# Landmark attention beside a feed-forward stream: two attention products on smaller array tiles, one conversion on more partitions, and a reordered slot table

## The chip, the cores and the metric

The kernel runs on one core of a Trainium2 chip. The metric is the device time of one execution in microseconds (us); the time before is the median of three runs. Times of instructions come from one profiled execution.

## The reference, cut to what matters

Three blocks follow one another on 8 batches of 576 positions and 512 features: attention through 32 landmarks per head (8 heads of 64), a feed-forward block with a low-rank mix over positions, and a second block with a Fourier mix.

```python
q_lm, k_lm = means of q and k over 18 positions each       # 32 landmarks
A  = softmax(q @ k_lm.T);  Bm = softmax(q_lm @ k_lm.T);  C = softmax(q_lm @ k.T)
Z  = Bm.T / (norm1(Bm) * norminf(Bm) + 1e-6)
for _ in range(6): Z = 2 * Z - Z @ Bm @ Z                  # Newton
x  = A @ Z @ C @ v                                         # attention
u  = x + (x.transpose @ U @ V).transpose                   # U: 576x32, V: 32x576
y  = u + relu(u @ w_ch1) @ w_ch2                           # 512 -> 2048 -> 512
# then the Fourier block, ending in another 512 -> 2048 -> 512
```

U, V and the weights arrive as 64-bit floats and are converted on the chip.

## The kernel before, in words

Each of the two 512-2048-512 products is done in two passes, with half of the hidden units each. A pass streams nine chunks of 512 positions (`Mlp.stream`). A chunk has 16 steps: in steps 0 to 7 `up` computes one block of hidden units (12 matmuls of 128x512, lines 241 to 243), steps 8 to 15 are halves of the four down blocks (12 matmuls each, lines 285 to 287). The numbers are split into a high and a low part, which makes three matmuls of one product.

The attention of the eight batches is interleaved with pass 0, and a few small steps of it stand after the matmuls of each step of the stream. `Batch.steps` gives each of them a slot number; `Slots` hangs them onto the steps, and within a slot they are issued in the order of the table. Every engine and the DMA queue on SyncE run their instructions in the order written (`manual_schedule`). Batch b starts 12 steps before chunk b-1, so slot r of it falls on step (r + 4) mod 16 of a chunk. Batch 0 and the first 12 slots of batch 1 lie in a prologue ahead of the first chunk, in which `filler` matmuls (line 962) stand in each slot.

The attention works on pairs of heads: k and q lie as head features on partitions 0 to 63 and 64 to 127. `scores(g)` (slots 6 and 8) multiplies landmark queries with all keys, two heads per half g, into two PSUM banks "c" of 288 columns; the maximum is taken on VectorE and the exponential on ScalarE. `newton` (slots 14 to 19) is one step of the iteration on eight 32x32 blocks. `query_t` and `query_tail` (slots 16, 17) transpose the softmax of the queries into the tile `at`. `heads` and `rank` (slots 20, 21) build the tile `W`. `mix(i)` (slots 22 to 25) is W times `at` for 128 output features: before, the contraction has 128 rows, of which 64 belong to two heads, 32 to the low-rank part (V lies there in `at`, and U'A times W in `W`), and 32 are zeros. Its two banks "n" are copied by ScalarE into a tile `u1T`, stored by a DMA of ScalarE, and split into high and low parts for the stream (`hand_head`).

The weights of pass 0 are converted one after the other by `convert`: five VectorE operations on 128x512 (lines 96, 97, 100, 103, 106), two on ScalarE, two on GpSimd. U and V go first through `from_f64` (lines 61 to 72). The generator `convs` chains them: two of its pieces per slot in the prologue from slot 4 on, four per step in chunk 0. The feed-forward needs weight i at step i.

Of the kernel before, what the change touches and what calls it, by code (L numbers as in the profile page):

```python
# [22 lines left out]
LM, W = 32, 18  # L23
# [16 lines left out]
def body(ctx: ExitStack, tc: tile.TileContext, qT, kT, vn, mU, mV, w11, w12, w21, w22,  # L40
# [273 lines left out]
    staged = [[dram.tile([P, 2, 512], F32, name=f"d{p}_{i}") for i in range(2 * HM)] for p in range(4)]  # L314
    BANKS = {"c": 2, "b": 1, "n": 2}

    def attention_constants(cp, t):
# [12 lines left out]
        nc.gpsimd.memset(t["at"][0:32, 1:4:2, :], 0.0)  # L330

    def attention_setup(t, pool, cvp):
        uraw = cvp.tile([P, 1024], U32, name="wraw", bufs=2)[:, 0:10 * R].bitcast(U64).rearrange(
            "p (t r) -> p t r", r=R)
        nc.sync.dma_start(uraw[:, 0:4, :], mU[0:512].rearrange("(t p) r -> p t r", p=P))
        for e in range(2):
            nc.sync.dma_start(uraw[64 * e:64 * e + 64, 4, :], mU[512:576])
        yield 1
        yield from from_f64(cvp, t["U"].rearrange("p t r -> p (t r)"), uraw.rearrange("p t r -> p (t r)"), 5 * R)
        vst = pool.tile([P, S], F32, name="u1T", bufs=2)[0:R]  # L340
        for n in range(3):
            c = slice(n * S // 3, (n + 1) * S // 3)
            vraw = cvp.tile([P, 1024], U32, name="wraw", bufs=2)[0:R, 0:2 * S // 3].bitcast(U64)
            nc.sync.dma_start(vraw, mV[:, c])
            yield 1
            yield from from_f64(cvp, vst[:, c], vraw, S // 3, R)
        for e in range(2):
            for g in range(2):
                nc.scalar.copy(t["at"][64 - 32 * e:96 - 32 * e, 2 * g + e, :], vst)
            yield 1  # L350

    class Batch:
# [100 lines left out]

        def scores(self, g):

            qb = self.t["qb"]
            E = self.E[g] = self.pool.tile([P, S], F32, name="E", bufs=2)
            m, s, x = self.stat(2), self.stat(2), self.stat(1)
            if g == 0:
                self.rC = self.stat(2)  # L460
            pss = []
            for n in range(2):
                ps = self.bank("c")
                for e in range(2):
                    nc.tensor.matmul(ps[self.EJ[e], 0:HS], qb[:, 2 * g + e, :],  # L465
                                     self.k[:, 2 * g + e, n * HS:(n + 1) * HS], start=True, stop=True)
                pss.append(ps)
            for n in range(2):
                nc.vector.tensor_reduce(m[:, n:n + 1], pss[n][:, 0:HS], axis=AX.X, op=ALU.max)
            nc.vector.tensor_scalar(x, m[:, 0:1], m[:, 1:2], -self.scC, op0=ALU.max, op1=ALU.mult)  # L470
            for n in range(2):
                nc.scalar.activation(E[:, n * HS:(n + 1) * HS], pss[n][:, 0:HS], AF.Exp, bias=x, scale=self.scC,
                                     accum_out=s[:, n:n + 1])
            r = self.rC[:, g:g + 1]
            nc.vector.tensor_scalar(r, s[:, 0:1], s[:, 1:2], 1e-9, op0=ALU.add, op1=ALU.add)
            nc.vector.reciprocal(r, r)

# [74 lines left out]
        def query_t(self, g):  # L552
            at = self.t["at"]
            ps = self.bank("c")
            for i in range(4):
                nc.tensor.transpose(ps[:, i * P:(i + 1) * P], self.A[:, 512 * g + i * P:512 * g + (i + 1) * P], ident_sb)
            nc.scalar.copy(at[0:64, 2 * g, 0:512], ps[0:64])
            nc.scalar.copy(at[64:P, 2 * g + 1, 0:512], ps[64:P])

        def query_tail(self):  # L560
            at = self.t["at"]
            ps = self.bank("b")
            for g in range(2):
                nc.tensor.transpose(ps[0:64, g * P:(g + 1) * P], self.A[:, 1024 + 64 * g:1088 + 64 * g], ident_sb)
            v = ps[0:64, 0:2 * P].rearrange("p (g c) -> p g c", g=2)
            nc.scalar.copy(at[0:64, 0:4:2, 512:S], v[:, :, 0:64])
            nc.scalar.copy(at[64:P, 1:4:2, 512:S], v[:, :, 64:P])

# [34 lines left out]
        def heads(self):  # L603
# [7 lines left out]
            v = ps[:, 0:P].rearrange("p (g c) -> p g c", g=2)  # L611
            for h in range(4):
                sl, e, c = slice(32 * h, 32 * h + 32), h // 2, slice(64 * (h % 2), 64 * (h % 2) + 64)
                if e:
                    nc.vector.tensor_copy(W_[sl, e:4:2, c], v[sl])
                else:
                    nc.scalar.copy(W_[sl, e:4:2, c], v[sl])

        def rank(self):
# [3 lines left out]
            for g in range(2):  # L623
                for e in range(2):
                    sl, o = self.EJ[e], slice(64 - 32 * e, 96 - 32 * e)
                    nc.tensor.matmul(ps[o, P * g:P * g + P], self.au[sl, g, :], W_[sl, 2 * g + e, :], start=True,
                                     stop=True)
            v = ps[:, 0:2 * P].rearrange("p (g c) -> p g c", g=2)
            nc.scalar.copy(W_[64:96, 0:4:2, :], v[64:96])
            nc.vector.tensor_copy(W_[32:64, 1:4:2, :], v[32:64])  # L630

        def mix(self, i):
            W_, at, u = self.t["W"], self.t["at"], u1[self.b]
            if self.b == 0:
                self.mlp.hand_tail(0, i)
            u1T = self.pool.tile([P, S], F32, name="u1T", bufs=2)
            pss = []
            for n in range(2):
                ps = self.bank("n")
                nc.tensor.matmul(ps[:, 0:HS], W_[:, i, :], at[:, i, n * HS:(n + 1) * HS], start=True, stop=True)  # L640
                pss.append(ps)
            nc.scalar.copy(u1T[:, 0:HS], pss[0][:, 0:HS])
            nc.scalar.copy(u1T[:, HS:S], pss[1][:, 0:HS])
            nc.scalar.dma_start(u[rows(i), :], u1T)
            self.mlp.hand_head(self.b, i, u1T)

        def steps(self, after):
# [15 lines left out]
            yield from ((22 + i, lambda i=i: self.mix(i)) for i in range(4))  # L663
            if after:
# [248 lines left out]
    with pool("mm") as mp, pool("pm", space=PSUM) as pm:  # L913
# [34 lines left out]
        with pool("aa") as ap_, pool("ac") as ac, pool("cv0") as cv0, pool("pt", space=PSUM) as psb:  # L948
# [139 lines left out]
```

## Time and profile before

| quantity | us |
|---|---|
| median of three runs (1944.62 to 1950.64) | 1946.72 |
| profiled execution | 1947.52 |
| its span, first to last instruction | 1945.7 |
| TensorE busy in the span | 1888.9 (97%) |
| VectorE busy | 932.1 (48%) |
| ScalarE busy | 554.7 (29%) |
| GpSimd busy | 372.0 (19%) |

The 1.8 us by which the profiled time exceeds its span lie around the first and the last instruction. Busy times overlap, and a matmul in the pipeline counts as busy until its modelled end. A matmul on 4-byte floats that aren't split shows as two rows of the trace: `mix(i)`, two matmuls in the program, is four rows.

### The profile page before, as it was taken

The numbers are of one execution on the slowest core, as the hardware profiler recorded it, in microseconds if no ns is written. First come the engines' busy times: TensorE is split into PE (matmuls) and PEld (weight loads), VectorE is DVE, ScalarE is ACT, GpSimd is POOL, SyncE is SP. The second block draws the span as 40 slices with busy tenths as digits, with TensorE's granted clock in tenths as the row PEclk, the third lists the DMA queues.
The fourth block names the chain that finished last, engine by engine and source line by source line (L and its number), as shares of the span: only waits on it lengthen the run. The fifth ranks groups of instructions, "written<-read, shape, count | busy, mean of one in ns | idle before, by whom it ended". The sixth has DMA issues, their size and how long they took to land.

```text
span 1945.7 us, 29294 instructions
## 1 busy us (share of the span) xinstructions
PE 1888.9 (97%) x11840; PEld 1531.0 (79%) x11840; DVE 932.1 (48%) x1636; ACT 554.7 (29%) x1173; POOL 372.0 (19%) x357
## 2 busy tenths in 40 slices
PE   6879999999999999999999999999999999999998
PEld 5656777777788887887888888888888888888887
DVE  6885566556432334556474364554522133333333
ACT  3433333333331222333233243433322211111110
POOL 2450122112111122123232132312211000010000
PEclk9999999999999999999999999999999999999999
DMA  6424435444346533444352852442422743223332
GB/s 242 142 74 152 153 114 172 158 149 139 102 133 210 179 114 128 143 147 165 128 163 85 301 173 79 136 157 85 146 92 97 233 134 110 93 92 98 98 98 76
DMA packets 150232, 267.14 MB, mean 137 GB/s; under 512 B 23536, under 2 KB 81744, under 8 KB 150096
## 3 DMA queue, kind: packets, MB, share of 16 engines
q1 hardware_dynamic: 145488, 255.82, 39.6%
q10 hardware_dynamic: 4608, 9.44, 1.3%
q8 instruction: 93, 1.52, 0.3%
q14 instruction: 43, 0.35, 0.1%
HBM read 171.62 MB, written 93.59 MB: 136 GB/s over the span
## 4 chain that ended last, share of the span: by engine, by line
PE 86%; DVE 7%; ACT 2%; DMA 2%; issue 1%; SPq 0%; ACTq 0%; POOL 0%; DVEq 0%
PE ps L285 13%; PE ps L287 13%; PE ps L286 13%; PE ps L241 12%; PE ps L243 12%; PE ps L242 12%; PE ps_n L640 1%; DMA U<-x 1%; PE ps_f L76 1%; PE ps_f L77 1%; PE ps_f L78 1%; DVE g L246 1%; PE ps_c L465 1%; PE ps L962 1%; DVE cva L106 1%
## 5 line engine op out<-in xcount | busy, mean ns | idle before, releaser
L285 PE MATMUL ps<-g,w 128*128 128x512 f32 x1152 | 461.7, 401 | 0.0
L241 PE MATMUL ps<-x,w 128*128 128x512 f32 x1152 | 459.4, 399 | 0.0
L287 PE MATMUL ps<-g,w 128*128 128x512 f32 x1152 | 451.1, 392 | 1.2 <-DVE g L246 1.2
L286 PE MATMUL ps<-g,w 128*128 128x512 f32 x1152 | 450.5, 391 | 0.0
L243 PE MATMUL ps<-x,w 128*128 128x512 f32 x1152 | 449.8, 390 | 0.0
L242 PE MATMUL ps<-x,w 128*128 128x512 f32 x1152 | 449.6, 390 | 0.0
L246 DVE SCALAR_TENSOR_TENSOR g<-ps,g 128x512 fp32r<-128x512 f32 x288 | 198.5, 690 | 476.2 <-ACT g L245 475.7
L245 ACT ACTIVATE g<-ps 128x512 fp32r<-128x512 f32 x288 | 171.8, 597 | 716.4 <-PE ps L243 716.0
L285 PEld LDWEIGHTS ps<-g,w 128*128 128x128 f32 x1152 | 217.1, 188 | 51.3 <-issue 5.9
L287 PEld LDWEIGHTS ps<-g,w 128*128 128x128 f32 x1152 | 217.2, 189 | 48.8 <-DVE g L246 2.1
L241 PEld LDWEIGHTS ps<-x,w 128*128 128x128 f32 x1152 | 216.5, 188 | 49.0 <-issue 0.3
L243 PEld LDWEIGHTS ps<-x,w 128*128 128x128 f32 x1152 | 216.5, 188 | 46.5
L286 PEld LDWEIGHTS ps<-g,w 128*128 128x128 f32 x1152 | 217.4, 189 | 43.5
L242 PEld LDWEIGHTS ps<-x,w 128*128 128x128 f32 x1152 | 216.8, 188 | 42.6
L294 DVE TENSOR_TENSOR xf<-ps,xf 128x512 f32<-128x512 f32 x108 | 74.5, 690 | 241.9 <-PE ps L287 210.1
L52 POOL TENSOR_TENSOR x<-xf,x 128x512 fp32r<-128x512 f32 (+7 forms) x70 | 85.5, 1228 | 529.0 <-ACT x L51 493.8
L104 POOL TENSOR_TENSOR cvp<-cvp,cva 128x512 f32<-128x512 f32 x64 | 85.8, 1341 | 401.7 <-DVE cvp L103 401.5
L52 POOL TENSOR_TENSOR stg<-cva,stg 128x512 fp32r<-128x512 f32 x48 | 68.3, 1424 | 98.6 <-ACT stg L51 98.0
L51 ACT CAST x<-xf 128x512 fp32r<-128x512 f32 (+7 forms) x140 | 75.1, 575 | 0.4
L101 ACT ACTIVATE wraw<-wraw 128x512 f32<-128x512 f32 x56 | 38.0, 678 | 97.8 <-DVE cva L97 97.8
L106 DVE SCALAR_TENSOR_TENSOR cva<-wraw,cvp 128x512 f32<-128x512 f32 x56 | 51.0, 911 | 29.6 <-POOL cvp L104 29.6
L52 DVE TENSOR_TENSOR x<-xf,x 128x512 fp32r<-128x512 f32 (+7 forms) x70 | 50.1, 715 | 29.9 <-ACT x L51 26.9
(278 smaller groups left out, 1745.8 us busy)
## 6 DMA issues: line engine op xcount, KB each, us to landing
wraw<-w SPq DMA_DIRECT2D x56, 512.0 KB
d<-stg SPq DMA_DIRECT2D x48, 512.0 KB
w<-d SPq DMA_DIRECT2D x48, 512.0 KB
y<-xf SPq DMA_DIRECT2D x72, 256.0 KB
xf<-y SPq DMA_DIRECT2D x72, 256.0 KB
u<-u1T ACTq DMA_DIRECT2D x32, 288.0 KB
U<-x SPq DMA_DIRECT2D x8, 1152.0 KB
u<-U SPq DMA_DIRECT2D x8, 1152.0 KB
```

The costliest lines, as they stand in the source:

```text
L51: nc.scalar.copy(hi, src)
L52: (eng or nc.vector).tensor_tensor(lo, src, f32(hi), op=ALU.subtract)
L104: nc.gpsimd.tensor_tensor(pf, pf, af, op=ALU.add)
L241: nc.tensor.matmul(ps, wh, xh, start=k == 0, stop=False)
L242: nc.tensor.matmul(ps, wl, xh, start=False, stop=False)
L243: nc.tensor.matmul(ps, wh, xl, start=False, stop=k == 3)
L245: nc.scalar.activation(g[:, 0, :], ps, AF.Relu)
L246: nc.vector.scalar_tensor_tensor(out=g[:, 1, :], in0=ps, scalar=0.0, in1=f32(g[:, 0, :]), op0=ALU.max, op1=ALU.subtract)
L285: nc.tensor.matmul(ps, wh, gh, start=k == 0, stop=False)
L286: nc.tensor.matmul(ps, wl, gh, start=False, stop=False)
L287: nc.tensor.matmul(ps, wh, gl, start=False, stop=k == HM - 1)
L294: nc.vector.tensor_tensor(res[d], ps, res[d], op=ALU.add)
```

## The change

`mix` becomes `mix(g, n)`: the zero rows go, each head pair gets a contraction of 64 rows (32 attention rows and 32 low-rank rows), and four matmuls of 64x64 by 288 columns write two banks. `scores` becomes one step (slot 6) for both halves, with contraction over one head's 64 features, 32 landmarks and 512 columns, on eight tiles of 64x32; the last 64 columns of all eight heads go to bank "b" as 128x32 tiles. `at` and `W` get a new layout, so `query_t` and `query_tail` copy in quarters of 32 partitions, and `rank` runs on 32x32 tiles. V is converted in one go on 96 partitions and put into `at` by twelve DMAs in slot 14. Newton's steps are first in their slots.

```diff
-        t["W"] = cp.tile([P, 4, P], F32, name="W")
-        nc.gpsimd.memset(t["W"], 0.0)
-        nc.gpsimd.memset(t["at"][96:P, 0:4:2, :], 0.0)
-        nc.gpsimd.memset(t["at"][0:32, 1:4:2, :], 0.0)
+        t["W"] = cp.tile([P, 4, 64], F32, name="W")
...
-        for n in range(3):
-            vraw = cvp.tile([P, 1024], U32, name="wraw", bufs=2)[0:R, 0:2 * S // 3].bitcast(U64)
-            nc.sync.dma_start(vraw, mV[:, c])
-            yield 1
-            yield from from_f64(cvp, vst[:, c], vraw, S // 3, R)
-        for e in range(2):
-            for g in range(2):
-                nc.scalar.copy(t["at"][64 - 32 * e:96 - 32 * e, 2 * g + e, :], vst)
-            yield 1
+        for n in range(3):
+            nc.sync.dma_start(vraw[R * n:R * n + R], mV[:, n * S // 3:(n + 1) * S // 3])
+        yield 1
+        yield from from_f64(cvp, t["vst"], vraw, S // 3, 3 * R)
+    def place_v(t):
+        for n in range(3):
+            src = t["vst"][R * n:R * n + R].unsqueeze(1).to_broadcast([R, 2, S // 3])
+            for h in range(4):
+                nc.sync.dma_start(t["at"][32 * h:32 * h + 32, 1 - h % 2:4:2, n * S // 3:(n + 1) * S // 3], src)
...
+            pss, tl = [self.bank("c") for _ in range(2)], self.bank("b")
+            for g in range(2):
+                for h, sl in enumerate(self.QUARTERS):
+                    r, c = self.EJ[h % 2 ^ g], slice(32 * (h % 2), 32 * (h % 2) + 32)
+                    nc.tensor.matmul(pss[g][sl], qb[r, 2 * g + h // 2, c], self.k[r, 2 * g + h // 2, 0:512], ...)
+            for g in range(2):
+                for h, sl in enumerate(self.QUARTERS):
+                    nc.tensor.matmul(tl[sl, 64 * g:64 * g + 64], qb[:, 2 * g + h // 2, c],
+                                     self.k[:, 2 * g + h // 2, 512:S], ...)
...
-            nc.scalar.copy(at[0:64, 2 * g, 0:512], ps[0:64])
-            nc.scalar.copy(at[64:P, 2 * g + 1, 0:512], ps[64:P])
+            for h, sl in enumerate(self.QUARTERS):
+                nc.scalar.copy(at[sl, 2 * g + h % 2, 0:512], ps[sl])
...
-        def mix(self, i):
-                nc.tensor.matmul(ps[:, 0:HS], W_[:, i, :], at[:, i, n * HS:(n + 1) * HS], start=True, stop=True)
+        def mix(self, g, n):
+            if n == 0:
+                self.u1T = [self.pool.tile([P, S], F32, name="u1T", bufs=UB) for _ in range(2)]
+            pss = [self.bank("n") for _ in range(2)]
+            for c, cl in enumerate(self.EJ):
+                for r, sl in enumerate(self.EJ):
+                    nc.tensor.matmul(pss[r][cl, 0:HS], W_[sl, 2 * g + c, :], at[sl, 2 * g + c, q], ...)
+            for r in range(2):
+                nc.scalar.copy(self.u1T[r][:, q], pss[r][:, 0:HS])
+            if n == 1:
+                for r in range(2):
+                    nc.scalar.dma_start(u[rows(i), :], self.u1T[r])
+                    self.mlp.hand_head(self.b, i, self.u1T[r])
...
-            yield from ((6, lambda: self.scores(0)), (8, lambda: self.scores(1)), (10, lambda: self.scores_t(0)),
+            yield from ((14 + i, lambda i=i: self.newton(i)) for i in range(6))
+            yield from ((6, self.scores), (10, lambda: self.scores_t(0)),
...
-            yield from ((14 + i, lambda i=i: self.newton(i)) for i in range(6))
...
+            slots.add(FIRST, [(14, lambda: place_v(t))])
```

Here `EJ` are the two halves of the partitions and `QUARTERS` the four quarters; UB is 3, so `u1T` has three buffers in place of two.

The program's order shows three places. The first is TensorE in the prologue, from batch 1's `scores` and batch 0's `heads` on (L962 are the fillers). Before:

```order
L609 MATMUL ps_n<-ry,Bf 32x64 x8
L465 MATMUL ps_c<-k__364,qb 64x288 x4
L962 MATMUL ps<-ident_sb 128x128 x6
L626 MATMUL ps_n<-W,au 32x128 x4
L962 MATMUL ps<-ident_sb 128x128 x6
L640 MATMUL ps_n<-at,W 128x288 x2
L431 MATMUL ps_b<-dg,bones_sb 128x128
L465 MATMUL ps_c<-k__364,qb 64x288 x4
```

The same place now:

```order
L617 MATMUL ps_n<-ry,Bf 32x64 x8
L463 MATMUL ps_c<-k__390,qb 32x512 x8
L468 MATMUL ps_b<-k__390,qb 32x64 x8
L971 MATMUL ps<-ident_sb 128x128 x6
L628 MATMUL ps_n<-W,au 32x64 x8
L971 MATMUL ps<-ident_sb 128x128 x6
L644 MATMUL ps_n<-at,W 64x288 x4
L430 MATMUL ps_b<-dg,bones_sb 128x128
```

The second `scores` (L465) is gone from the step of `norms` (L431, now L430), the first has become L463 and L468, and `mix` has four matmuls instead of two.

The second place is VectorE in the prologue after `residue` (L450, now L449; lines 61 to 72 are U and V, 96 to 106 the weights, 507 and 536 belong to `values` and `query`). Before:

```order
L450 SCALAR_TENSOR_TENSOR ry<-ps_b,st,istack_sb 128x32 x2
L61 TENSOR_SCALAR cva<-wraw 32x192
L62 SCALAR_TENSOR_TENSOR cva<-wraw,cva 32x192
L65 TENSOR_SCALAR cvp<-cva 32x192
L68 SCALAR_TENSOR_TENSOR cvp<-wraw,cvp 32x192
L72 SCALAR_TENSOR_TENSOR u1T<-wraw,cvp 32x192
L61 TENSOR_SCALAR cva<-wraw 32x192
L62 SCALAR_TENSOR_TENSOR cva<-wraw,cva 32x192
L507 TENSOR_TENSOR st<-st 128x2
```

Now:

```order
L72 SCALAR_TENSOR_TENSOR u1T<-wraw,cvp 96x192
L449 SCALAR_TENSOR_TENSOR ry<-ps_b,st,istack_sb 128x32 x2
L96 TENSOR_SCALAR cva<-g 128x512
L97 SCALAR_TENSOR_TENSOR cva<-g,cva 128x512
L100 TENSOR_SCALAR cvp<-cva 128x512
L103 SCALAR_TENSOR_TENSOR cvp<-g,cvp 128x512
L96 TENSOR_SCALAR cva<-g 128x512
L97 SCALAR_TENSOR_TENSOR cva<-g,cva 128x512
L106 SCALAR_TENSOR_TENSOR cva<-g,cvp 128x512
L100 TENSOR_SCALAR cvp<-cva 128x512
L103 SCALAR_TENSOR_TENSOR cvp<-g,cvp 128x512
L543 TENSOR_REDUCE sm<-ps_c 128x16
```

V is finished here, and the weights follow at once; before, they began six slots further on. Five weights were finished (L106) ahead of the first hidden block (L246), now eight.

The third place is VectorE at the end of the conversions in chunk 0. Before, the last of the 16 (L106 without a further L96) stands in step 10, between two down blocks (L294):

```order
L294 TENSOR_TENSOR xf<-ps,xf 128x512
L630 COPY W<-ps_n 32x2x128
L52 TENSOR_TENSOR x<-xf,x 128x64
L408 TENSOR_REDUCE st<-ps_b 128x2
...
L469 TENSOR_REDUCE st<-ps_c 128x1 x2
L470 TENSOR_SCALAR st<-st 128x1
L475 TENSOR_SCALAR st<-st 128x1
L476 RECIPROCAL st<-st 128x1
L106 SCALAR_TENSOR_TENSOR cva<-wraw,cvp 128x512
L294 TENSOR_TENSOR xf<-ps,xf 128x512
```

Now it stands behind the last hidden block (L246), which ends step 7:

```order
L246 SCALAR_TENSOR_TENSOR g<-ps,g 128x512
L608 TENSOR_TENSOR ry<-ps_n,ry 128x2x64
L383 TENSOR_REDUCE ls<-q__1343 128x64
L106 SCALAR_TENSOR_TENSOR cva<-wraw,cvp 128x512
L619 COPY W<-ps_n 128x256
L52 TENSOR_TENSOR x<-xf,x 128x64
L294 TENSOR_TENSOR xf<-ps,xf 128x512
```

Steps 8 to 15 of chunk 0 hold no conversion any more.

## Rows read from the trace of the kernel before

**Rows 1.** The profile's first part: span, and busy time of TensorE

```profile
span 1945.7 us, 29294 instructions
PE 1888.9 (97%) x11840; PEld 1531.0 (79%) x11840; DVE 932.1 (48%) x1636; ACT 554.7 (29%) x1173; POOL 372.0 (19%) x357
```

**Rows 2.** Busy time by stretch (stretch, length, PE, PEld, DVE, ACT, POOL, clock, DMA)

```profile
20.00:30.00 10.00, 10.00 (x221) 9.26 (x221) 4.45 (x18) 3.16 (x9) 0.58 (x1) 1.00 0.38 131
79.00:123.00 44.00, 34.58 (x494) 26.07 (x492) 36.98 (x67) 16.82 (x36) 20.49 (x18) 0.96 0.41 134
123.00:169.00 46.00, 38.12 (x202) 26.92 (x199) 29.09 (x64) 16.25 (x43) 14.77 (x16) 0.89 0.30 104
169.00:234.00 65.00, 64.98 (x689) 49.29 (x688) 36.35 (x82) 23.08 (x61) 10.68 (x16) 1.00 0.42 133
```

**Rows 3.** Waits of TensorE, first 160 us (total, times, longest)

```profile
PE ps_n L595 <- DVE ry L600: 10.4, 6, 3.1
PE ps_n L640 <- ACT u1T L642: 3.8, 2, 2.6
```

**Rows 4.** Groups of VectorE instructions from 79 to 151 us (busy, mean ns)

```profile
L106 DVE SCALAR_TENSOR_TENSOR cva<-wraw,cvp 128x512 f32<-128x512 f32 x8 | 5.6, 705 | 0.0
L97 DVE SCALAR_TENSOR_TENSOR cva<-wraw,cva 128x512 uint32<-128x512 uint32 x8 | 5.5, 693 | 0.3
L103 DVE SCALAR_TENSOR_TENSOR cvp<-wraw,cvp 128x512 f32<-128x512 uint32 x8 | 5.5, 692 | 0.3
L100 DVE TENSOR_SCALAR cvp<-cva 128x512 uint32<-128x512 uint32 x11 | 4.6, 419 | 0.0
```

**Rows 5.** VectorE in order of time: two operations on V, the last conversion

```profile
16.69 0.23 DVE L61 TENSOR_SCALAR cva<-wraw 32x192 uint32<-32x192 uint32 x1
16.96 0.35 DVE L62 SCALAR_TENSOR_TENSOR cva<-wraw,cva 32x192 uint32<-32x192 uint32 x1
...
149.96 0.67 DVE L106 SCALAR_TENSOR_TENSOR cva<-wraw,cvp 128x512 f32<-128x512 f32 x1
```

**Rows 6.** TensorE in order of time around a `mix` alone (start, length)

```profile
346.48 0.39 PE L287 MATMUL ps<-g,w 128*128 128x512 f32 x1
346.71 1.13 PE L640 MATMUL ps_n<-at,W 128*128 128x288 f32 x4
...
347.91 0.39 PE L286 MATMUL ps<-g,w 128*128 128x512 f32 x1
```

**Rows 7.** The same view around `mix` and `scores` in one step

```profile
341.45 0.39 PE L287 MATMUL ps<-g,w 128*128 128x512 f32 x1
341.67 1.13 PE L640 MATMUL ps_n<-at,W 128*128 128x288 f32 x4
342.74 1.19 PE L465 MATMUL ps_c<-k__3322,qb 128*64 128x288 f32 x8
...
344.19 0.40 PE L286 MATMUL ps<-g,w 128*128 128x512 f32 x1
```

**Rows 8.** The same view: 32x32 tiles, `newton` alone and a product of `residue`

```profile
311.52 0.39 PE L243 MATMUL ps<-x,w 128*128 128x512 f32 x1
311.84 0.53 PE L595 MATMUL ps_n<-ry 32*32 32x96 f32 x16
...
312.64 0.39 PE L242 MATMUL ps<-x,w 128*128 128x512 f32 x1
...
356.76 0.33 PE L447 MATMUL ps_b<-BT 32*32 32x32 f32 x16
```

**Rows 9.** The same view: `rank` on two 64x32 tiles, then `kernel`

```profile
337.99 0.63 PE L626 MATMUL ps_n<-W,au 64*32 64x128 f32 x8
338.54 0.33 PE L402 MATMUL ps_b<-kb,qb 128*32 128x32 f32 x16
```

**Rows 10.** ScalarE copies into `at` and one exponential of `scores`

```profile
L557 ACT COPY at<-ps_c x16: 563/566/577, 43.4 to 521.7; 64x512 f32<-64x512 f32 x16
...
345.58 0.50 ACT L472 ACTIVATE E<-ps_c,st 128x288 f32<-128x288 f32 x1 [1.54 <-DVE st L470]
```

More of the change, by code (lines that the diff above doesn't have):

```diff
@@ L315, in body @@
     BANKS = {"c": 2, "b": 1, "n": 2}
+    UB = 3
     def attention_constants(cp, t):
@@ L452, in residue, with scores @@
                                                op1=ALU.add)
-        def scores(self, g):
+        def scores(self):
             qb = self.t["qb"]
[L457 to L476, printed above, removed]
@@ new lines, in scores @@
+            for g in range(2):
+                for h, sl in enumerate(self.QUARTERS):
+                    c = slice(32 * (h % 2), 32 * (h % 2) + 32)
+                    nc.tensor.matmul(tl[sl, 64 * g:64 * g + 64], qb[:, 2 * g + h // 2, c],
+                                     self.k[:, 2 * g + h // 2, 512:S], start=True, stop=True, skip_group_check=True)
+            for g in range(2):
+                nc.vector.tensor_reduce(m[:, 0, g:g + 1], pss[g], axis=AX.X, op=ALU.max)
+            nc.vector.tensor_reduce(m[:, 1, :], tl[:, 0:P].rearrange("p (g c) -> p g c", g=2), axis=AX.X, op=ALU.max)
@@ new lines, in scores @@
+            nc.vector.tensor_tensor(x, m[:, 0, :], m[:, 1, :], op=ALU.max)
+            nc.vector.tensor_scalar_mul(x, x, -self.scC)
+            for g in range(2):
+                E = self.E[g] = self.pool.tile([P, S], F32, name="E", bufs=2)
+                nc.scalar.activation(E[:, 0:512], pss[g], AF.Exp, bias=x[:, g:g + 1], scale=self.scC,
+                                     accum_out=sm[:, 0, g:g + 1])
+                nc.scalar.activation(E[:, 512:S], tl[:, 64 * g:64 * g + 64], AF.Exp, bias=x[:, g:g + 1],
+                                     scale=self.scC, accum_out=sm[:, 1, g:g + 1])
@@ L478, in scores_t @@
+            nc.vector.tensor_tensor(self.rC, sm[:, 0, :], sm[:, 1, :], op=ALU.add)
+            nc.vector.tensor_scalar_add(self.rC, self.rC, 1e-9)
+            nc.vector.reciprocal(self.rC, self.rC)
         def scores_t(self, g):
@@ L563, in query_tail @@
             for g in range(2):
[L564 to L567, printed above, removed]
+                for e, sl in enumerate(self.EJ):
+                    nc.tensor.matmul(ps[sl, 64 * g:64 * g + 64], self.A[:, 1024 + 64 * g:1088 + 64 * g],
+                                     ident_sb[:, sl], start=True, stop=True)
+            for h, sl in enumerate(self.QUARTERS):
+                nc.scalar.copy(at[sl, h % 2:4:2, 512:S], ps[sl, 0:P].rearrange("p (g c) -> p g c", g=2))
         def mixed(self):
@@ L610, in heads @@
                                      start=True, stop=True, skip_group_check=True)
[L611 to L617, printed above, removed]
+            nc.vector.tensor_copy(W_.rearrange("p (g c) d -> p g c d", c=2),
+                                  ps[:, 0:P].rearrange("p (g d) -> p g d", g=2).unsqueeze(2).to_broadcast([P, 2, 2, 64]))
         def rank(self):
@@ L623, in rank @@
             for g in range(2):
[L624 to L630, printed above, removed]
-        def mix(self, i):
+                for h, sl in enumerate(self.QUARTERS):
+                    nc.tensor.matmul(ps[self.QUARTERS[h ^ 1], 64 * g:64 * g + 64], self.au[sl, g, :],
+                                     W_[sl, 2 * g + h % 2, :], start=True, stop=True, skip_group_check=True)
@@ L633, in mix @@
+            for h, sl in enumerate(self.QUARTERS):
+                (nc.vector.tensor_copy if h // 2 else nc.scalar.copy)(
+                    W_[sl, 1 - h % 2:4:2, :], ps[sl, 0:P].rearrange("p (g d) -> p g d", g=2))
+        def mix(self, g, n):
             W_, at, u = self.t["W"], self.t["at"], u1[self.b]
             if self.b == 0:
[L635 to L639, printed above, removed]
-                nc.tensor.matmul(ps[:, 0:HS], W_[:, i, :], at[:, i, n * HS:(n + 1) * HS], start=True, stop=True)
-                pss.append(ps)
@@ L642, in mix @@
[L642 to L645, printed above, removed]
+                self.mlp.hand_tail(0, 2 * g + n)
+            if n == 0:
+                self.u1T = [self.pool.tile([P, S], F32, name="u1T", bufs=UB) for _ in range(2)]
+            q = slice(n * HS, (n + 1) * HS)
+            pss = [self.bank("n") for _ in range(2)]
+            for c, cl in enumerate(self.EJ):
+                for r, sl in enumerate(self.EJ):
+                    nc.tensor.matmul(pss[r][cl, 0:HS], W_[sl, 2 * g + c, :], at[sl, 2 * g + c, q], start=True,
+                                     stop=True)
@@ L662, in steps @@
                 yield from ((20 + k // 2, lambda k=k: self.mlp.hand_tail(self.b, k)) for k in range(4))
-            yield from ((22 + i, lambda i=i: self.mix(i)) for i in range(4))
+            yield from ((22 + 2 * g + n, lambda g=g, n=n: self.mix(g, n)) for g in range(2) for n in range(2))
             if after:
```

19 lines of the change are left out of this document (13 added, 6 removed).

## The prediction

> **What bounds the kernel now.** I read the page's first part first: TensorE is busy in 97% of the span [rows 1], so where it never waits, only what its instructions cost counts. Then the busy times by stretch, to find where it does wait [rows 2]. The last two stretches differ: chunk 1 (169 to 234 us) has TensorE busy for 64.98 of 65 us, and VectorE and ScalarE have room. Chunk 0 (79 to 169 us) takes 90 us for the same 192 matmuls; TensorE is idle for 9.4 us in its first half and 7.9 us in its second, where the granted clock is also down to 0.89, and VectorE is busy for 37 of the 44 us of the first half. So there are two regimes: the prologue and chunk 0, bound by VectorE, which converts weights; and chunks 1 to 6, bound by TensorE. The waits agree: six waits of Newton's matmuls for VectorE, 10.4 us, lie in the first 160 us, and the two of `mix` for ScalarE [rows 3]. The change touches both regimes, and I cost them apart.
>
> **Regime 1: the conversions.** One weight costs VectorE 0.42 + 0.69 + 0.42 + 0.69 + 0.71 = 2.93 us (L96 is the same operation on the same size as L100) [rows 4]. V cost three rounds of five operations between 0.23 and 0.35 us [rows 5], some 4.5 us. An estimate: since each partition still holds 192 numbers, a round on 96 partitions costs the same 1.5 us, 3 us less in all. As the order shows, the room goes to weights: eight instead of five are finished before the first hidden block, and the last one at the end of step 7 instead of in step 10.
>
> Second half of chunk 0: it lasted 46 us, against 32.5 for half of chunk 1 [rows 2], and the last conversion ended at 149.96 us [rows 5], well inside it. Without conversions there I expect it to run as in a later chunk: 13.5 us less.
>
> First half: four pieces of a conversion per step as before, so 44 us as before. Newton's addition now stands ahead of the softmax work in VectorE's slot, so its matmul waits less; but VectorE does the same work in sum, and where it is the bound, order gains nothing. I take 0 for this edit (0 to 3 us gain).
>
> Prologue: VectorE gets three weights more, 8.8 us, and loses 3 us of V and about 1 us by the merged `scores`: 4.8 us more. It had idle time to take some of it: busy for 4.45 of the 10 us from 20 to 30 us [rows 2], just where the weights now begin. I take 2.5 us later; from 1 us earlier, if the idle time takes it all, to 5 us later. ScalarE loses four copies of V. The twelve DMAs of `place_v` stand on SP's queue ahead of a weight load, but seven of the first eight weights are loaded before them, and `mix` reads V eight slots later; I cost them at nothing, and 1 us in the bound if the next load comes late. The memsets that go lie beside the first loads: nothing.
>
> Sum of regime 1: -13.5 + 2.5 = **-11 us**, from -17 to -5.
>
> **Regime 2: a batch in steady state.** The matmuls of the stream start every 0.23 us [rows 6]. A small step costs the time from the last stream matmul before it to the second one behind it, less two such intervals (the first one behind it still waits for the pipeline).
> - `mix` alone: 347.91 - 346.48 - 0.46 = 0.97 us for four rows [rows 6], which is 0.84 ns per column and row, with nothing left for changing over.
> - Newton alone, 16 rows of 96 columns on 32x32 tiles: 312.64 - 311.52 - 0.46 = 0.66 us [rows 8]. Sixteen rows of 32 columns span 0.33 us, of 96 columns 0.53 us: 0.20 us for 64 columns is 0.195 ns per column and row, a quarter of 0.84. So four tiles on the diagonal do run side by side, and 0.66 - 0.30 = 0.36 us is the price of going to small tiles and back. An extra change of tile shape I estimate at a third of that, 0.13 us.
> - `mix` and `scores(0)`: 344.19 - 341.45 - 0.46 = 2.28 us, so one `scores` is 1.31 us [rows 7].
>
> Now the new ones, if all tiles of a set overlap. `mix(g, n)`: 8 rows of 288 columns on four tiles, 8 x 288 x 0.84 / 4 = 0.48 us, and 0.36: 0.84. `scores`: 16 rows of 512 columns on eight tiles, 0.86 us; its tail, 16 rows of 64 columns on four tiles, 0.22 us. By step of a chunk:
> - step 10: 2.28 becomes 0.48 + 0.86 + 0.22 + 0.36 + 0.26 = 2.18, -0.10
> - step 12: `mix` and `scores(1)`, 2.28, become 0.84: -1.44 (`norms` stays)
> - step 11: -0.13; step 13, where the 32x32 tiles of `residue` follow and a change of shape was paid anyhow: 0.97 + 0.36 becomes 0.48 + 0.36 + 0.13, -0.36
> - `rank`: 8 rows on two tiles took 338.54 - 337.99 = 0.55 us [rows 9]; now 16 rows of 64 columns on 32x32 tiles, 0.20, in the same shape as `kernel` behind it: -0.3
> - `query_tail` as real products, a change of shape more: +0.27; `values` behind `query(0)` saves one change: -0.13
>
> That is -2.2 us per batch. Six of the chunks (0 to 5) hold a `mix` and a `scores`, chunk 6 a `mix` alone (-0.5): **-14 us**.
>
> What hides the rest? ScalarE copies `at` in quarters: eight copies of 0.57 us [rows 10] instead of four, 2.3 us more, and `query_tail` two more; ScalarE is busy for 23 of 65 us [rows 2], so by share this is covered. By place it is tight: in step 5 the four copies and four small ones end some 3.4 us after the transposes, and `mixed`, which needs bank "b", comes 3.5 us after them (twelve stream matmuls, Newton's, and the changes of shape). The merged exponentials (two of 512 columns, longer than the 0.50 us of 288 [rows 10], and two of 64) stand ahead of the copies of `mix(0, 1)` on ScalarE, and `mix(1, 0)` waits for those banks; I count about 1 us to spare.
>
> **Sum.** 1947.5 - 11 - 14 = 1922.5 us for the profiled execution, which stands 0.8 us above the median of the runs shown. With 1 us for the tight places I predict 1923.
>
> The trace of before never shows two tiles that share columns but not rows, as the four of `mix` do in pairs. Its nearest rows are the diagonal tiles [rows 8], fully side by side, and `rank` on two of 64x32: 0.55 us for 8 x 128 x 0.84 = 0.86 us of columns [rows 9], so two at a time as well. I take full overlap; the other end is no overlap between the two row halves.
>
> A second doubt is the bank. In each half of `scores`, tiles of both row halves write one bank. Newton's diagonal tiles do that too, with four row groups, and run four at a time [rows 8]. The Trainium skill, page "TensorEngine Tiling (Array Packing)", section "Restrictions and Gotchas", says that different row tiles cannot access the same PSUM bank simultaneously. By that rule the row halves of `scores` would take turns. The trace disagrees for 32x32 tiles, and shows none of 64x32 that mix as many.
>
> **The rivals.**
> - Row halves on the same columns take turns. Then `mix` is 0.96 + 0.36 = 1.32 us and the eight tiles of `scores` need 1.72: 2.8 us more per batch than forecast, so a batch loses 0.6 us; with chunk 6, +5 instead of -14, in all 1941.5. Nothing shows it, but nothing in the trace excludes it: 0.13.
> - Only tiles that write one bank take turns: `scores` costs 0.86 us more, six times, 1928. Against it speak the diagonal tiles [rows 8]: 0.07.
> - Slower. The 64-row tiles run one after the other, whatever their place: `mix` then is 1.94 + 0.36 = 2.3 us, +1.33 four times, and `scores` 6.9 us in place of 0.86; that is 5.8 and 6.0 us above the forecast, so a batch costs 9.6 us more instead of 2.2 less; with chunk 6 the time is about 2000. The kernel gets slower than before once a batch loses over 1.8 us, which eats the 11 us of regime 1 in six batches; that is, once the tiles run less than about 1.6 at a time in `mix` and 3.2 in `scores`. `rank` [rows 9] speaks against it: 0.05.
> - ScalarE becomes the wait of steps 6 and 12 (`mixed`, `mix(1, 0)`), about 1.5 us per batch: 1932. Its share of 23 in 65 us speaks against more: 0.10.
>
> **How the numbers follow.** The forecast has 0.65; its own range is 1914 to 1934 (regime 1 by its bounds, regime 2 by 4 us). The rivals inside it change little; the first one ends at 1941.5, so the range of 8 in 10 is 1911 to 1940: it leaves out the slower rival, most of the first, and a tail below. Three thousandths, about what a measurement of this kernel can tell from no change, are 5.8 us, so "faster" means under 1941: the forecast, the bank and ScalarE, and a part of the first rival, 0.86. "Same" is the rest of the first and half-failures in regime 1: 0.09. Slower: 0.05.
>
> **What would show it.** Right: chunk 1 begins near 157 us instead of 168.5; the last L106 ahead of the down blocks ends near 126 us; the four waits of Newton in chunk 0 shrink; `mix(g, n)` spans less than 1 us in eight rows; a chunk with both lasts 2 us less than 65. Wrong: eight rows of `mix` spanning 1.3 us or more (row halves take turns); `scores` near 2.4 us with a fast `mix` (the bank); waits of `mixed` or `mix` for ScalarE in every chunk; or the first hidden block starting later than 85 us.

## The result, and the profile after

The changed kernel takes 1924.49 us (median of four runs, 1922.64 to 1925.51) against 1945.67 for the kernel before on the same chip: a ratio of 0.9887, 95% interval 0.9873 to 0.9901. The forecast was 1923, so the sum is right within 1.5 us. Its parts are not all right, and that the sum came out so close is partly luck; the experiments show where.

The profiled execution has a span of 1923.7 us, 22.0 less than before [rows 1]. The profile's first part, after:

```profile
span 1923.7 us, 30061 instructions
PE 1871.5 (97%) x12208; PEld 1508.9 (78%) x12208; DVE 923.4 (48%) x1610; ACT 567.9 (30%) x1207; POOL 368.3 (19%) x352
```

The share of 97% hasn't moved, and tells nothing. The busy times by stretch do (the columns of [rows 2]); the stretches are the halves of chunk 0, chunk 1 and chunk 2:

```profile
81.20:128.50 47.30, 37.32 (x500) 28.02 (x498) 39.40 (x73) 20.97 (x45) 21.66 (x20) 0.86 0.45 151
128.50:158.20 29.70, 29.70 (x241) 20.99 (x236) 15.57 (x42) 11.01 (x34) 5.43 (x7) 1.00 0.30 103
158.20:224.90 66.70, 64.66 (x735) 47.32 (x734) 37.08 (x81) 24.95 (x64) 10.68 (x16) 0.97 0.40 130
224.90:287.50 62.60, 62.60 (x735) 45.92 (x733) 38.39 (x85) 25.21 (x65) 12.37 (x17) 1.00 0.49 166
```

The second half of chunk 0 went from 46 us to 29.7, with TensorE never idle in it and its clock back at 2.4 GHz (1.00). The first half got longer, from 44.0 to 47.3. Chunk 1 is longer than any chunk of [rows 2], at 66.7, and chunk 2 is what was forecast, 62.6. Where the 22 us lie, by the starts of the chunks:

| part | before | after | difference | forecast |
|---|---|---|---|---|
| prologue | 78.98 | 81.19 | +2.2 | +2.5 |
| chunk 0, first half | 44.0 | 47.3 | +3.3 | 0 |
| chunk 0, second half | 45.6 | 29.75 | -15.9 | -13.5 - 2.2 |
| chunks 1 to 6 | 389.0 | 378.1 | -10.9 | -11.5 |
| all after | 1388.2 | 1387.4 | -0.8 | 0 |

(The forecast's regime 2 counts one batch of 2.2 us in chunk 0; its `mix` and `scores` stand in the second half, so the 2.2 belong there.)

VectorE in order of time shows why the second half is free: V's round on 96 partitions has about the durations of one round on 32 (0.26 and 0.35 us against 0.23 and 0.35 [rows 5]), and the last conversion is 18 us earlier:

```profile
18.66 0.26 DVE L61 TENSOR_SCALAR cva<-wraw 96x192 uint32<-96x192 uint32 x1
18.95 0.35 DVE L62 SCALAR_TENSOR_TENSOR cva<-wraw,cva 96x192 uint32<-96x192 uint32 x1
...
131.58 0.68 DVE L106 SCALAR_TENSOR_TENSOR cva<-wraw,cvp 128x512 f32<-128x512 f32 x1
```

TensorE in order of time around the new products, in a steady chunk (start, length, as in [rows 6, 7]):

```profile
329.84 0.39 PE L287 MATMUL ps<-g,w 128*128 128x512 f32 x1
330.16 0.71 PE L644 MATMUL ps_n<-at,W 64*64 64x288 f32 x8
330.80 1.09 PE L463 MATMUL ps_c<-k__3408,qb 64*32 64x512 f32 x16
331.82 0.43 PE L468 MATMUL ps_b<-k__3408,qb 128*32 128x64 f32 x16
...
338.75 0.71 PE L644 MATMUL ps_n<-at,W 64*64 64x288 f32 x8
339.40 0.49 PE L430 MATMUL ps_b<-dg,bones_sb 128*128 128x128 f32 x2
```

From `mix` to what follows it are 0.64 and 0.65 us: 0.48 of columns and 0.17 for the change of shape. `scores` takes 331.82 - 330.80 = 1.02 us: 0.86 and 0.16. All four, and all eight, tiles run side by side.

TensorE's waits in the first 160 us, against [rows 3]:

```profile
PE ps_n L603 <- DVE ry L608: 13.0, 6, 5.3
...
PE ps_n L644 <- ACT W L631: 2.4, 1, 2.4
PE ps_b L586 <- ACT at L575: 1.9, 1, 1.9
```

`mix` no longer waits for ScalarE's copies into `u1T`; its one wait for ScalarE, 2.4 us in the prologue, is for `rank`'s copy into `W`. Newton's matmuls wait longer than before, with one wait of 5.3 us.

### The profile page after: what moved, and what is told of

Same layout as the page of the kernel before. It is cut to its first block, busy times and chain, and to the rows that moved or that the text cites. A ratio compares the mean times of both kernels' runs of the same rounds, so it can differ in the third digit from the quotient of the medians.

```text
span 1923.7 us, 30061 instructions
## 1 busy us (share of the span) xinstructions
PE 1871.5 (97%) x12208; PEld 1508.9 (78%) x12208; DVE 923.4 (48%) x1610; ACT 567.9 (30%) x1207; POOL 368.3 (19%) x352
## 4 chain that ended last, share of the span: by engine, by line
PE 86%; DVE 7%; DMA 3%; ACT 2%; issue 1%; SPq 0%; ACTq 0%; DVEq 0%
PE ps L285 13%; PE ps L287 13%; PE ps L286 13%; PE ps L241 12%; PE ps L243 12%; PE ps L242 12%; PE ps_f L76 1%; DMA U<-x 1%; PE ps_f L77 1%; PE ps_f L78 1%; PE ps_n L644 1%; PE ps_n L603 1%; DVE g L246 1%; PE ps_c L532 1%; DVE cva L106 1%
## 5 line engine op out<-in xcount | busy, mean ns | idle before, releaser
L246 DVE SCALAR_TENSOR_TENSOR g<-ps,g 128x512 fp32r<-128x512 f32 x288 | 198.5, 690 | 491.7 <-ACT g L245 491.1
L294 DVE TENSOR_TENSOR xf<-ps,xf 128x512 f32<-128x512 f32 x108 | 74.5, 690 | 254.3 <-PE ps L287 225.4
L106 DVE SCALAR_TENSOR_TENSOR cva<-wraw,cvp 128x512 f32<-128x512 f32 x56 | 49.6, 885 | 28.9 <-POOL cvp L104 28.9
```

The lines of the kernel that those rows point to most:

```text
L246: nc.vector.scalar_tensor_tensor(out=g[:, 1, :], in0=ps, scalar=0.0, in1=f32(g[:, 0, :]), op0=ALU.max, op1=ALU.subtract)
L294: nc.vector.tensor_tensor(res[d], ps, res[d], op=ALU.add)
```

## The experiments

Ratios are to the kernel before, timed on the same chip; the changed kernel, run once more in the third set, has 0.9892 (0.9878 to 0.9905) there, at 1925.39 us.

### Does V's round count for its 3 us, or for when the weights begin?

`v_three`: V in three rounds on 32 partitions again, the rest of the change kept.

```diff
-        yield from from_f64(cvp, t["vst"], vraw, S // 3, 3 * R)
+        for n in range(3):
...
+            yield from from_f64(cvp, t["vst"][:, c], vraw, S // 3, R)
+        yield from wait(2)
...
```

> The changed kernel, with V converted in three rounds on 32 partitions as before (still placed by DMAs, two slots later). Two regimes (my theory): the weights begin and end as late as before the change, chunk 1 begins near 168 us instead of 158, and the time is 1924.5 + 10 = 1934 us (1930 to 1938). Tiles alone (rival: the whole gain comes from TensorE's shorter steps, the conversions lie beside other work): 1925 us. Newton's order (rival: chunk 0 got shorter because Newton's additions stand first): 1925 us, chunk 1 near 158 us.

`v_pause`: the single round stays, but the weights begin as late as with three.

```diff
         yield from from_f64(cvp, t["vst"], vraw, S // 3, 3 * R)
+        yield from wait(12)
...
```

> The changed kernel, with twelve empty pieces behind V's single round (and V placed two slots later): VectorE is spared the 3 us of V's work as in the change, but the weights begin as late as before. If the earlier begin is what counts (more weights fit into the prologue's idle time and fewer stand in chunk 0): 1932 us, chunk 1 near 166 us. If the 3 us of saved work are what counts: at most 1928 us, chunk 1 at 161 us or earlier.

`v_only`: the kernel before with V's single round and late placing alone.

```diff
...
-            yield from from_f64(cvp, vst[:, c], vraw, S // 3, R)
...
-                nc.scalar.copy(t["at"][64 - 32 * e:96 - 32 * e, 2 * g + e, :], vst)
...
+        yield from from_f64(cvp, t["vst"], vraw, S // 3, 3 * R)
...
+            slots.add(FIRST, [(14, lambda: place_v(t))])
```

> The kernel before, with nothing but V's single round on 96 partitions and its placing by DMAs. Two regimes: chunk 1 begins 10 us earlier, at about 159 us, chunks last as before, 1945.7 - 10 = 1936 us (1933 to 1940). Tiles alone: 1945 us, no difference. If the two parts work on each other (merged scores and shorter mix make the earlier conversions possible): 1940 us or more.

Measured: `v_three` 1930.32 us, 0.9914 (0.9902 to 0.9927); `v_pause` 1932.27, 0.9921 (0.9908 to 0.9934); `v_only` 1941.31, 0.9969 (0.9958 to 0.9980). The first two lie together, though one does 3 us of VectorE's work less: what counts is when the weights begin. (The first conversion starts at 23.3 us in the changed kernel, at 42.3 in `v_three`, at 44.6 in `v_pause` and at 41.7 before the change.) Both give back less than the 10 us that I had expected of `v_three`. The halves of chunk 0 in `v_pause`, by stretch:

```profile
81.20:125.80 44.60, 37.30 (x500) 28.04 (x498) 39.22 (x73) 21.27 (x45) 21.64 (x20) 0.89 0.41 136
125.80:166.75 40.95, 34.87 (x241) 23.49 (x237) 24.79 (x57) 14.32 (x40) 13.80 (x13) 0.87 0.33 112
```

The second half is 41.0 us instead of 29.75, and the first 44.6 instead of 47.3. Early weights take 11 us off one half and put 3 onto the other; in the time, the two undone versions cost 5 and 7 us (0.0027 and 0.0034 of 1946), or 4 and 6 against the 0.9892 of the third set. And in `v_only`:

```profile
83.75:131.10 47.35, 38.62 (x493) 29.01 (x491) 35.80 (x66) 16.88 (x36) 20.43 (x18) 0.86 0.45 144
131.10:166.87 35.77, 33.57 (x204) 25.22 (x197) 18.22 (x49) 12.49 (x36) 6.75 (x10) 0.95 0.27 90
```

The same first half of 47.35 us, but 35.8 in the second, where the old `mix` still stands and `heads` waits 2.2 us for Newton's result, and a prologue of 83.75. In this execution, the slowest of its seven, V's round alone brings chunk 1 forward by only 1.7 us. The time falls in the third branch of what was expected (1940 us or more), but it does not show that the parts need each other: alone V's round gains 6.0 us (0.0031), and taking it out again costs about as much.

### Is Newton's order worth nothing?

`newton_last` puts Newton's steps behind the others again in the changed kernel; `newton_only` puts them first in the kernel before; `newton_v` does so in `v_only`.

```diff
+            yield from ((14 + i, lambda i=i: self.newton(i)) for i in range(6))
             yield from ((6, lambda: self.scores(0)), (8, lambda: self.scores(1)), (10, lambda: self.scores_t(0)),
...
-            yield from ((14 + i, lambda i=i: self.newton(i)) for i in range(6))
             yield from ((20, self.heads), (21, self.rank))
```

(The diff is that of `newton_only`.)

> The changed kernel, with Newton's steps at their old place in the slot table, last in their slots. My theory says order gains nothing while VectorE is the bound and TensorE waits for nothing later: 1924.5 us within 1.5 us, the waits of Newton's matmuls in chunk 0 somewhat longer, those of the matmuls behind them shorter. Newton's order (rival): 1930 us or more.

> The kernel before, with nothing but Newton's steps first in their slots. Taking them last again cost the changed kernel 4 us at the begin of chunk 1 and 2.2 us of waits in later chunks. If that is a gain of its own: chunk 1 at 164.5 us instead of 168.5, no wait of Newton after it, 1945.7 - 6 = 1939.5 us. My recorded zero: 1945 us within 2. If it counts only where the weights end early (their end still holds up the second half of chunk 0 here): 1943 us, the 2.2 us of the later chunks alone.

> The kernel before, with V's single round and Newton's steps first, both without any new tiling. If the two effects add: V's round alone began chunk 1 at 166.9 us, less 4 us for Newton's order is 163 us, and with 2.2 us of later waits 1933 to 1936 us. If the tilings are needed for V's round to pay (the prologue, 4.8 us longer with V's round alone, is held up by the two separate scores): chunk 1 at 165 us or later, 1938 us.

Measured: `newton_last` 1931.69 us, 0.9925 (0.9911 to 0.9938); `newton_only` 1940.00, 0.9965 (0.9952 to 0.9977); `newton_v` 1935.06, 0.9940 (0.9926 to 0.9953). The edit gives 6.7 us by itself, undoing it costs some 7 (6 against the 0.9892), and with V's round it nearly adds up: 11.7 us together, 6.0 and 6.8 apart. My zero falls. In the changed kernel the greater part of the gain lies in chunk 0, whose halves in `newton_last` are:

```profile
81.46:130.72 49.26, 39.34 (x499) 29.74 (x497) 37.00 (x68) 20.52 (x43) 20.66 (x18) 0.83 0.43 145
130.72:162.24 31.52, 29.82 (x243) 21.04 (x237) 18.20 (x47) 11.71 (x35) 6.40 (x9) 1.00 0.29 98
```

They are 2.0 and 1.8 us longer than in the changed kernel, and chunk 1 begins 4.0 us later. In `newton_only` the gain lies elsewhere: of the 6.6 us of span, 1.0 is in chunk 0 and most of the rest in chunks that I had called bound by TensorE. Chunk 4 of the kernel before, by stretch:

```profile
363.70:431.30 67.60, 64.98 (x687) 49.04 (x686) 37.99 (x83) 22.79 (x59) 10.20 (x16) 1.00 0.51 174
```

and chunks 2 and 4 of `newton_only`:

```profile
232.30:296.80 64.50, 64.50 (x689) 48.87 (x687) 38.55 (x87) 22.89 (x60) 12.47 (x17) 1.00 0.48 168
361.30:425.80 64.50, 64.50 (x688) 48.87 (x686) 37.95 (x83) 22.91 (x59) 10.21 (x16) 1.00 0.54 183
```

Chunks 1 to 5 before are 64.7, 65.7, 64.7, 67.7 and 64.7 us; with Newton first all five are 64.5, 5.0 us less: 1.1 in chunk 2, 3.2 in chunk 4, and 0.2 in each of the others, where TensorE waits for nothing before either. The waits of TensorE from 160 to 600 us say which ones went. Before:

```profile
PE ps_c L525 <- issue: 2.3, 2, 1.3
PE ps_n L595 <- DVE ry L600: 2.2, 2, 1.3
```

In `newton_only` Newton's waits are gone, and of the first line one pause of 1.0 us is left.

### What makes chunk 1 longer?

In chunk 1 of the changed kernel VectorE, in order of time, does this:

```profile
206.94 0.16 DVE L481 TENSOR_TENSOR st<-st 128x2 f32<-128x2 f32 x1 [2.17 <-ACT E L479]
...
207.43 0.41 DVE L96 TENSOR_SCALAR cva<-wraw 128x512 uint32<-128x512 uint32 x1
207.87 0.69 DVE L97 SCALAR_TENSOR_TENSOR cva<-wraw,cva 128x512 uint32<-128x512 uint32 x1
208.59 0.43 DVE L100 TENSOR_SCALAR cvp<-cva 128x512 uint32<-128x512 uint32 x1
209.06 0.69 DVE L103 SCALAR_TENSOR_TENSOR cvp<-wraw,cvp 128x512 f32<-128x512 uint32 x1
209.67 0.68 DVE L294 TENSOR_TENSOR xf<-ps,xf 128x512 f32<-128x512 f32 x1
...
211.96 0.57 DVE L423 TENSOR_TENSOR dg<-istack_sb,st 128x128 f32<-128x128 f32 x1
```

and TensorE's waits from 160 to 560 us, with its busy times at the place (columns of [rows 2]), are:

```profile
PE ps_b L430 <- DVE dg L423: 2.8, 2, 2.0
```

```profile
212.50:214.00 1.50, 1.41 (x5) 1.22 (x6) 1.22 (x5) 0.62 (x1) 0.14 (x1) 0.57 0.10 34
214.00:217.40 3.40, 3.40 (x15) 2.42 (x13) 1.50 (x3) 0.00 (x0) 1.14 (x1) 0.69 0.02 5
217.40:221.00 3.60, 3.60 (x37) 2.62 (x37) 1.57 (x4) 1.73 (x4) 0.94 (x1) 1.00 0.61 155
```

The sum of the exponentials (L481) stands right behind `scores` in VectorE's order and holds everything behind it for 2.17 us, the pieces of `norms` (L423) among them. So `norms`' matmul comes 2.0 us late, and after that pause the granted clock is 0.57 and then 0.69, partly at 1.2 GHz, before it is 1.00 again. The same wait of 2.17 us stands in every later chunk, mostly without harm. In chunk 2:

```profile
273.40 0.16 DVE L481 TENSOR_TENSOR st<-st 128x2 f32<-128x2 f32 x1 [2.17 <-ACT E L479]
...
273.88 0.67 DVE L294 TENSOR_TENSOR xf<-ps,xf 128x512 f32<-128x512 f32 x1
...
275.55 0.74 DVE L423 TENSOR_TENSOR dg<-istack_sb,st 128x128 f32<-128x128 f32 x1
```

Here L423 starts 2.15 us behind L481, in chunk 1 it is 5.02, because pieces of a weight's conversion (L96 to L103, 2.2 us) stand between them. So it takes the wait and the conversion together to make `dg` that late. In chunk 4, with one piece between them (L106), TensorE waits for the other 0.8 us of that line. `late_sums` moves the three small operations to the start of `scores_tail`, where the sums have long been there:

```diff
-            nc.vector.tensor_tensor(self.rC, sm[:, 0, :], sm[:, 1, :], op=ALU.add)
-            nc.vector.tensor_scalar_add(self.rC, self.rC, 1e-9)
-            nc.vector.reciprocal(self.rC, self.rC)
+            self.smC = sm
...
         def scores_tail(self):
+            nc.vector.tensor_tensor(self.rC, self.smC[:, 0, :], self.smC[:, 1, :], op=ALU.add)
...
```

> The changed kernel, with the three small VectorE operations on the softmax sums of scores moved from behind the exponentials (slot 6) to scores_tail (slot 11). They wait 2.17 us for ScalarE there, and everything behind them on VectorE waits along. If that wait is what made dg late for norms in chunk 1 (2.0 us, and a chunk 4 us longer than the forecast), it goes: chunk 1 at 62.6 us like its neighbours and the prologue 1 to 2 us shorter, 1919 us. Rival: the staging work in chunk 1 made dg late, and VectorE has room elsewhere: 1924 us.

Measured: 1917.63 us, 0.9862 (0.9847 to 0.9877). Chunks 1 and 2, by stretch:

```profile
153.78:217.00 63.22, 62.86 (x736) 45.94 (x733) 36.50 (x81) 24.71 (x64) 10.45 (x16) 1.00 0.42 139
217.00:279.60 62.60, 62.60 (x736) 45.92 (x733) 38.29 (x85) 25.18 (x65) 12.30 (x17) 1.00 0.50 165
```

Chunk 1 is 63.2 instead of 66.7, with the clock at 1.00, and the wait for `dg` is gone, although the conversion still stands in chunk 1. The prologue ends at 76.45 instead of 81.19, 4.7 us earlier, where I had expected 1 to 2: the same wait of VectorE stands there twice.

`scores_two` goes the other way and takes `scores` of the kernel before, two halves in slots 6 and 8, into the changed one:

```diff
...
-            yield from ((6, self.scores), (10, lambda: self.scores_t(0)),
+            yield from ((6, lambda: self.scores(0)), (8, lambda: self.scores(1)), (10, lambda: self.scores_t(0)),
```

> The changed kernel, with scores as in the kernel before (two steps in slots 6 and 8, 128x64 tiles, contraction over 128 rows with zeros). By the trace step 12 of a chunk gets 1.3 to 1.45 us longer and step 10 stays: six times 1.4 is 8.5 us; the wait of norms in chunk 1 may go (2 to 4 us back): 1924.5 + 8.5 - 3 = 1930 us (1927 to 1933). If eight tiles didn't overlap, as the rule on one bank says, the old form would be no slower: 1924 us or less.

Measured: 1928.65 us, 0.9919 (0.9904 to 0.9933). Chunks 1 and 2:

```profile
160.50:224.50 64.00, 63.74 (x720) 46.52 (x717) 36.45 (x83) 24.93 (x64) 10.73 (x16) 1.00 0.42 136
224.50:288.20 63.70, 63.70 (x720) 46.56 (x717) 38.88 (x87) 25.43 (x66) 11.85 (x17) 1.00 0.49 165
```

A steady chunk is 1.1 us longer, and chunk 1 is 2.7 shorter: the merged `scores` gains in each chunk and brought most of the stall of chunk 1 with it.

### What makes the first half of chunk 0 longer?

VectorE's waits in the first 160 us of the changed kernel name a load of raw weights; VectorE and the queue on SP, in order of time:

```profile
DVE cva L96 <- DMA wraw<-w: 2.5, 1, 2.5
```

```profile
94.63 0.68 DVE L106 SCALAR_TENSOR_TENSOR cva<-wraw,cvp 128x512 f32<-128x512 f32 x1
...
102.36 0.43 DVE L96 TENSOR_SCALAR cva<-wraw 128x512 uint32<-128x512 uint32 x1 [2.55 <-DMA wraw<-w]
```

```profile
95.39 0.34 SPq L88 DMA_DIRECT2D wraw<-w  x1
```

The load goes out at 95.39 us, as soon as the L106 of two weights earlier has freed its buffer (94.63 + 0.68), and VectorE has to wait for it until 102.36; at 106.80 follows Newton's wait of 5.3 us. The conversions had caught up with the loads, which have two raw buffers. `v_only`, with early weights too, has the same wait (3.3 us). `raw3` gives three buffers, and fetches one weight further ahead (the weights staged in later chunks, and U and V, share them); `raw3_late` adds `late_sums`.

```diff
...
-                        raw = cv0.tile([P, 1024], U32, name="wraw", bufs=2)
+                        raw = cv0.tile([P, 1024], U32, name="wraw", bufs=3)
...
-                if len(raws) < EARLY or len(raws) < i + 2:
+                if len(raws) < EARLY or len(raws) < i + 3:
```

> The changed kernel, with three instead of two buffers for the raw weights in pass 0, and loads one weight further ahead. In chunk 0 VectorE waited 2.55 us for a raw weight, and TensorE 5.3 us for Newton behind it. If the two buffers are the cause, that wait goes and the first half of chunk 0 falls from 47 to 44 us: 1921 us. Rival: VectorE is full there anyhow, what it doesn't wait here it waits for later: 1924 us.

> Both of the preceding edits, three raw buffers and the sums later: if both waits are real and apart, their gains add: 1916 us. If one hides the other: 1919 us. If neither counts: 1924 us.

Measured: `raw3` 1921.82 us, 0.9883 (0.9869 to 0.9898); `raw3_late` 1915.25, 0.9851 (0.9835 to 0.9868). The first two stretches of `raw3`:

```profile
81.90:125.20 43.30, 36.31 (x500) 27.11 (x498) 38.02 (x70) 20.47 (x43) 21.64 (x20) 0.92 0.44 153
125.20:155.02 29.82, 29.82 (x241) 21.04 (x237) 16.43 (x44) 11.62 (x35) 5.39 (x7) 1.00 0.30 102
```

The first half is 43.3 us instead of 47.3, VectorE's wait for the load is no longer in the list, and Newton's longest wait is 3.1. In the timed runs that gain alone is not told from nothing (0.9883 against 0.9887, the intervals overlap); in the profile chunk 1 begins 3.2 us earlier. With the later sums it is: `raw3_late` and `late_sums` ran in one set, and all runs of the first (1913.06 to 1916.40 us) lie below all of the second (1916.78 to 1918.98). I had expected 1916 if both gains add.

The pair was run once more beside the changed kernel, on one chip.

> The changed kernel itself, unchanged, beside the others on one chip: 1924.5 us within 2, ratio to the kernel before 0.989.

> Three raw buffers and the later sums once more, beside the changed kernel on one chip: 1915 us, 9 us less than the changed kernel, so that both gains stand against it directly.

Measured: the changed kernel 1925.39 us; with both edits 1915.21, 0.9839 (0.9825 to 0.9852), 10.2 us less. That version beats both kernels.

## Why the prediction was right, and where it was not

**Regime 2, one batch: right within 0.3.** Forecast -2.2 us per steady chunk; chunk 3 went from 64.74 to 62.58, -2.16. But 0.2 of that is Newton's order (64.5 in `newton_only`), so the tiles gave 1.9. By step, forecast and measured: step 10 -0.10 and -0.06, step 11 -0.13 and -0.13, step 12 -1.44 and -1.44, step 13 -0.36 and -0.32, `rank` (step 9) -0.3 and -0.20, `query_tail` (step 5) +0.27 and +0.30, `values` (step 0) -0.13 and -0.14. The estimate of 0.13 for a change of shape measures 0.16 to 0.17.

**Rivals of the array: refuted.** If row halves took turns, `mix` would need 0.96 us of columns, and `scores` 1.72; from start to start they take 0.64 and 1.02, with the change of shape. The rule of the bank falls in the form in which I quoted it: in each half of `scores`, tiles of both row halves write one bank, on different partitions, and eight run at once in 1.02 us. The Trainium skill, page "TensorEngine Tiling (Array Packing)", section "Restrictions and Gotchas", says that different row tiles cannot access the same PSUM bank simultaneously; here the measurement decides against it for tiles whose outputs lie on different partitions. Two row halves that write the same partitions of one bank were not tried: `mix` gives them two banks.

**ScalarE: right.** The one wait of `mixed` for `at` is 1.9 us in chunk 0, where it was 2.8 before the change; in later chunks there is none.

**Regime 2, the sum: right by two errors.** Chunks 1 to 6 gave 10.9 us, forecast 11.5. Clean chunks gave 1.9 each against those of `newton_only` (64.5 to 62.6), 9.6 in five. Newton's order gave 5.0 more in the same five, which I had priced at nothing. Three chunks took 5.5 back (66.7, 63.4 and 63.1 instead of 62.6): 4.3 of that goes with `late_sums`, in chunks 1 and 4, so that much is the merged sums; 0.6 in chunk 1 stays, and so does chunk 5, where TensorE pauses for nothing that the profile shows (0.4 us, and 1.0 in `late_sums`). In chunk 6 the 1.8 us are mostly a pause of 1.0 us at `query` that is gone. The failed steps: "order gains nothing" was argued for the stretch where VectorE is the bound, and it does not hold even there (4.0 us in chunk 0 of the changed kernel, by `newton_last`); and I let chunk 1 stand for all of chunks 1 to 6 and never asked what Newton's order does in the later ones, although the trace held 2.2 us of Newton's waits there. And I counted where the exponentials delay ScalarE's copies, but not what stands behind L481 on VectorE, which waits for them.

**Regime 1, second half: right in its mechanism, the number helped by luck.** Forecast -15.7 with its batch, measured -15.9. `v_pause` shows that the main cause is the end of the conversions, but that is worth 11.2 us and not 13.5. The other 4.7 are the tiles and Newton's order, 1.8 of it by `newton_last`, where I had 2.2.

**Regime 1, first half: wrong by 3.3.** The step "four pieces of a conversion per step as before, so 44 us as before" left out that conversions that begin earlier also ask for their loads earlier. I had looked at the load ahead of `place_v` only, with 1 us in the bound. The two raw buffers are the limit; `raw3` returns 4.0 us. Newton's order hid a part of the loss: without it this half lasts 49.3 us.

**Prologue: right number, reason not shown.** I gave +2.5 for 4.8 us more of VectorE's work; it is +2.2. The work was priced too low: a weight takes VectorE 3.6 us in the first 78 us of the changed kernel (0.55 + 1.05 + 0.65 + 0.69 + 0.69, the mean of each operation), not the 2.93 of chunk 0. In the kernel before, early weights lengthen the prologue by 4.8 us (`v_only`, 83.75) or 4.4 (83.60 in `newton_v` against 79.22 in `newton_only`), so its idle time took nothing. In the changed kernel they cost 0 to 1.9: with late weights chunk 0 starts at 81.18 in `v_pause` and at 79.30 in `v_three`, against 81.19. Nor did the waits of VectorE for the exponentials grow: they are 4.3 us in the prologue and were 4.8 before. Without them the prologue is 4.7 us shorter (76.45 in `late_sums`). How these combine to +2.2 is open.

**The sum as a whole: luck.** By whole edits, in time, the early weights with V's round are worth 4 to 7 us (`v_three`, `v_pause`, `v_only`), for which I had 11; Newton's order 6 to 7, for which I had nothing; and the rest, which is the smaller tiles with what the merged `scores` costs, 9 to 10 (0.9940 in `newton_v` against 0.9887 and 0.9892), for which I had 14. The order that I priced at nothing made up for two terms that I priced too high.

**What I named as signs.** Chunk 1 begins at 158.25 (I said 157), the last L106 is at 131.58 (126; `raw3` has it at 129.34, so the load is a part of it). Newton's waits in the first half of chunk 0 did not shrink, from 6.6 to 8.0 us; in `raw3` they are 5.0, so the load hid it.

## What to carry to other kernels

Price a reordering at every place where the trace has a wait of the moved step, not only in the stretch that it seems made for: waits of about 1 us in two later chunks, and 0.2 us in each, were worth half as much as the smaller tiles in all of them. When a step that produces on one engine is merged or made longer, look at the instruction that consumes it on an in-order engine and at all that is queued behind that; moving three tiny operations later was worth 5 to 7 us (0.9862 against 0.9887 and 0.9892; 0.9851 against 0.9883), in the profile about half of it in the prologue. When work is moved earlier, check that its loads and their buffers move as well.

## What the runs showed of the hardware

Eight 64x32 tiles over both row halves run side by side, with four of them per bank: 16 rows of 512 columns in 1.02 us. A change between small shapes measures 0.16 to 0.17 us. A pause of TensorE of 2.0 us was followed by 4.9 us at a mean granted clock of 0.57 and 0.69, so partly at 1.2 GHz; chunk 1 lost 4.1 us for a wait of 2.0. An estimate of what the clock took of the rest, from the lengths and clocks of those two stretches, is 1.50 x 0.43 + 3.40 x 0.31 = 1.7 us; it was not measured by itself.
